# Late gates and their slot table moved ahead of the next unit's x on VectorE

## The chip, the cores and the metric

The kernel runs on one core of one Trainium2 chip. The metric is device time in microseconds of one execution, given as the median of several runs; lower is better. The kernel before takes 718.80 us (three runs: 718.79, 718.80 and 719.53).

## The reference

Three layers follow each other. Banded attention (4 batches, 8 heads, 576 positions, 64 channels; half of the heads see the last 32 positions, the others every fourth of the last 128) gives `x`, 2304 tokens by 512. A dense layer maps `x` through 2048 hidden units with a squared ReLU. A mixture of 8 experts then takes every token to the one expert with the largest logit and scales its output by a gate:

```python
logits = xn @ en.T / tau
expert_idx = np.argmax(logits, axis=1)
probs = np.exp(logits - logits.max(-1, keepdims=True))
probs /= probs.sum(-1, keepdims=True) + 1e-09
gate_w = probs[np.arange(N), expert_idx]
for e in range(E):
    mask = expert_idx == e
    h = np.maximum(x[mask] @ w1[e], 0.0)
    out[mask] = gate_w[mask, None] * (h @ w2[e])
```

(`xn` and `en` are the tokens and expert vectors divided by their norms; 512 inputs, 1024 hidden units for each expert.)

## The kernel before, in words

Attention and the dense layer take the first part of the span; tokens are worked on in five groups, and the last group (`g = 4`, four tiles of 128 tokens) is ready last. The routing decides which expert each token belongs to and sorts tokens into slots of 128 places. Slots are worked on in *units*: a pair of slots with one expert's weights, or a single slot. Unit 0 (slots 0 to 3, two passes) is formed early from the first four groups; all later units need the whole routing, which `slot_table` writes out as tables: which token is gathered into which place (`gidx`), where its output row goes (`sidx`), and its gate.

For one unit, `xt` transposes the gathered tokens on TensorE into a bank `px` (`x_turn`, L1123) and splits them into a high and a low half (`x_out`: ScalarE writes `xh`, L1135, VectorE `xl`, L1136). `g1_pair` multiplies them with the first weights into `ph` in four parts of 24 matmuls; ScalarE and VectorE make `hh` and `hl` of each part (L1159, L1160). `g2` multiplies those with the second weights into `po`, scales by the gate (L1205) and scatters the rows (L1206). Each matrix product is three matmuls of split operands (`mm3`, L468 to 470). The weights come as eight tiles `raw[k]` by DMA from the SyncE queue (L1084 for k under 4, L1086 for the others), and `split` turns each into `wh` (ScalarE, L1101) and `wl` (VectorE, L1102). A `raw[k]` is loaded again, for the next unit, when its `wl` is done.

The gates of the last group are made late, by `gates_late`: an inverse norm (L713 to 730), a product (L847), an Exp on ScalarE (L849), a sum (L850, L851), a reciprocal (L853) and the split of the gate into three bf16 numbers in `g3` (L854 to 857). Three products of the slot marks `eq` with the three rows of `g3` give `gb` (L919, 18 tiles by 25 places). 18 small matmuls on TensorE (`finish`, L925) sum `gb` into `pgate`, and a reduction (L928) gives the gate of each slot place. `finish` stands in TensorE's program between the last `g2` of unit 0 (slot 3) and the `g1` of unit 1 (slots 4 and 5).

TensorE runs its instructions in the order in which the code issues them. On VectorE and ScalarE a scheduler sets the order in this part of the program (after L1364 of the kernel before, in the loop over units, it is the code's order); `tc.issue_after(ins)` keeps what is issued under it behind `ins` on its engine. Each engine works its queue in order.

Of the kernel before, what the change touches and what calls it, by code (L numbers as in the profile page):

```python
# [11 lines left out]
AF = mybir.ActivationFunctionType  # L12
# [99 lines left out]
class Kern:  # L112
# [729 lines left out]
    def gates(self, g, ssq):  # L842
        nc, lp, n = self.nc, self.lpool, GT[g]
        sl = slice(T0[g], T0[g] + n)
        L = self.rel[:, sl, :]
        rn = self.inv_norm(lp, ssq[:, :n], n, f"yn{g}")
        nc.vector.tensor_mul(L, L, rn.unsqueeze(2).to_broadcast([P, n, NE]))  # L847
        z = lp.tile([P, 4], F32, tag="lz", name=f"lz{g}", bufs=2)[:, :n]
        nc.scalar.activation(L, L, AF.Exp)  # L849
        nc.vector.tensor_reduce(out=z, in_=L, axis=AX.X, op=ALU.add)  # L850
        nc.vector.tensor_scalar_add(z, z, 1e-9)  # L851
        gt = lp.tile([P, 4], F32, tag="lgt", name=f"lgt{g}", bufs=2)[:, :n]
        nc.vector.reciprocal(gt, z)  # L853
        nc.vector.tensor_copy(self.g3[:, 0, sl], gt)  # L854
        nc.vector.tensor_sub(z, gt, self.g3[:, 0, sl])
        nc.vector.tensor_copy(self.g3[:, 1, sl], z)
        nc.vector.tensor_sub(self.g3[:, 2, sl], z, self.g3[:, 1, sl])
# [6 lines left out]
    def bc(self, x, w):  # L864
        return x.unsqueeze(2).to_broadcast([P, x.shape[1], w])
# [17 lines left out]
    def slot_table(self, pos, nt, ns, nm):  # L883
        nc, pool, bc = self.nc, self.rpool, self.bc
        pi = pool.tile([P, 3, NTT], I32, tag="pi", name=f"pi{nm}")[:, :, :nt]
        pf = pool.tile([P, 2, NTT], F32, tag="pf", name=f"pf{nm}")[:, :, :nt]
        nc.vector.tensor_copy(pi[:, 0], pos)
        nc.vector.tensor_scalar(out=pi[:, 1], in0=pi[:, 0], scalar1=7, scalar2=None, op0=ALU.arith_shift_right)
        nc.vector.tensor_scalar(out=pi[:, 2], in0=pi[:, 0], scalar1=127, scalar2=None, op0=ALU.bitwise_and)
        nc.vector.tensor_copy(pf, pi[:, 1:3])  # L890
        eq = pool.tile([P, NTT * NPOS], F32, tag="eq", name=f"eq{nm}")[:, :nt * ns].rearrange("p (t j) -> p t j", t=nt)
        bt = pool.tile([P, NTT * 3 * NPOS], BF16, tag="bt", name=f"bt{nm}")[:, :nt * 2 * ns].rearrange(
            "p (t a j) -> p t a j", t=nt, a=2)
        nc.vector.tensor_tensor(out=eq, in0=bc(pf[:, 0], ns), in1=self.iota_j[:, :ns].unsqueeze(1).to_broadcast([P, nt, ns]),
                                op=ALU.is_equal)
        for i in range(2):
            nc.vector.tensor_mul(bt[:, :, i], eq, bc(self.dig[:, i, :nt], ns))
        pt = self.bank(f"ptab{nm}")
        at = pool.tile([P, NTT, P], BF16, tag="at", name=f"at{nm}")
        for t in range(nt):  # L900
            nc.vector.tensor_scalar(out=at[:, t], in0=self.iota_r, scalar1=pf[:, 1, t:t + 1], scalar2=None, op0=ALU.is_equal)
            nc.tensor.matmul(pt[:, 0:2 * ns], lhsT=at[:, t], rhs=bt[:, t].rearrange("p a b -> p (a b)"),
                             start=(t == 0), stop=(t == nt - 1))
        tb = pool.tile([P, 2, NPOS], F32, tag="tb", name=f"tb{nm}")[:, :, :ns]
        nc.vector.tensor_copy(tb, pt[:, 0:2 * ns].rearrange("p (a b) -> p a b", a=2))
        tk = pool.tile([P, NPOS], F32, tag="tk", name=f"tk{nm}")[:, :ns]
        nc.vector.scalar_tensor_tensor(out=tk, in0=tb[:, 0], scalar=64.0, in1=tb[:, 1], op0=ALU.mult, op1=ALU.add)
        gidx = pool.tile([P, ns], U32, name=f"gidx{nm}")
        self.last_gidx = nc.vector.tensor_scalar(out=gidx, in0=tk, scalar1=-1.0, scalar2=0.0, op0=ALU.add, op1=ALU.max)

        def rest():
            em = pool.tile([P, NPOS], F32, tag="em", name=f"em{nm}")[:, :ns]
            nc.vector.tensor_scalar(out=em, in0=tk, scalar1=0.0, scalar2=8192.0, op0=ALU.is_equal, op1=ALU.mult)
            sidx = pool.tile([P, ns], U32, name=f"sidx{nm}")
            nc.vector.scalar_tensor_tensor(out=sidx, in0=tk, scalar=-1.0, in1=em, op0=ALU.add, op1=ALU.add)
            gb = pool.tile([P, NTT * 3 * NPOS], BF16, tag="bt", name=f"gb{nm}")[:, :nt * 3 * ns].rearrange(
                "p (t a j) -> p t a j", t=nt, a=3)
            for i in range(3):
                nc.vector.tensor_mul(gb[:, :, i], eq, bc(self.g3[:, i, :nt], ns))  # L919
            return lambda: finish(sidx, gb)  # L920

        def finish(sidx, gb):
            pg = self.bank(f"pgate{nm}")
            for t in range(nt):
                nc.tensor.matmul(pg[:, 0:3 * ns], lhsT=at[:, t], rhs=gb[:, t].rearrange("p a b -> p (a b)"),  # L925
                                 start=(t == 0), stop=(t == nt - 1))
            gate = pool.tile([P, ns], F32, name=f"gate{nm}")
            nc.vector.tensor_reduce(out=gate, in_=pg[:, 0:3 * ns].rearrange("p (a b) -> p b a", a=3), axis=AX.X, op=ALU.add)  # L928
            return sidx, gate
        return gidx, rest  # L930
# [353 lines left out]
    def experts(self):  # L1284
        nc, tc = self.nc, self.tc
        w, xs, xts = self.w, self.xs, {}
# [6 lines left out]
        runs, place, n = [[]], {}, NEARLY  # L1293
# [39 lines left out]
        def gather(r):  # L1333
            for j in runs[r]:
                xs[j] = self.gather(j)

        def xt(r):
            xts[r] = self.xt(runs[r], [xs.pop(j) for j in runs[r]])
# [4 lines left out]
        gi, rest = tables()  # L1343
# [6 lines left out]
        part(3)  # L1350
        with tc.issue_after(self.last_gidx.ins):
            self.gates_late()
        self.g2(2, 0, *hts, w[0])
        xt(1)
        behind.append((self.last_xl,))
        for a in range(2):
            with ExitStack() as st:
# [3 lines left out]
                    self.split(1, k, w[1])  # L1361
        load_for(2)
        gather(2)
        rest = rest()  # L1364
        self.g2(3, 1, *hts, w[0])
        si, ga = rest()
        for j, p in place.items():
# [14 lines left out]
        with tc.manual_schedule(engines={mybir.EngineType.Activation, mybir.EngineType.DVE}):  # L1382
            raws, u = [self.raw, []], 1
            while u < nstat:
# [5 lines left out]
                ahead = None  # L1390
                for i in range(4):
                    if i == (u == 1):
                        if more:
                            ahead = self.x_turn(runs[u + 1], [xs.pop(j) for j in runs[u + 1]], True)
# [103 lines left out]
```

## Time and profile before

| | |
|---|---|
| time, median of 3 runs | 718.80 us |
| the profiled execution's own time | 719.62 us |
| its span, first to last instruction | 717.9 us |
| around the span | 1.7 us |
| TensorE busy in the span | 701.7 us, 98% |
| VectorE / ScalarE busy | 71% / 52% |
| mean granted TensorE clock | 0.994 of full |

Times in the profile are microseconds from the span's start. A busy share is an average; what a change in one stage is worth is read from that stage's rows. PE is TensorE's matmul, DVE is VectorE, ACT ScalarE, POOL GpSimd and SPq SyncE's queue of DMA issues. The idle time in square brackets is what an engine waited just before a group, with what ended it; a group with `x3` is three instructions in a row, with the time from the first one's start to the last one's end. TensorE's clock has two levels, 2.4 GHz (shown as 1.00) and 1.2 GHz (0.50).

### The profile page before, as it was taken

To read this page: it belongs to the slowest core of one execution; us is meant where nothing else is said; L and a number is where in the kernel's file an instruction comes from. 1 tells how busy PE (TensorE), PEld (TensorE's weight loads), DVE (VectorE), ACT (ScalarE), POOL (GpSimd) and SP (SyncE) were. 2 spreads that over 40 slices of the span, in tenths; PEclk is the share of its full clock that TensorE was granted. 3 is DMA by queue.
4 is the path that set the end of the run, shared out by engine and by line. 5 is a ranking of instruction groups with operands and counts; after the bars stand their busy time and mean duration, and the time that the engine had idled before them with its cause. 6 is when DMAs were issued, how large, how long until landed. Compare 5 with 4: busy or idle time off the path is not lost. (4 is left out here: it accounts for less than half of the span.)

```text
span 717.9 us, 13286 instructions
## 1 busy us (share of the span) xinstructions
PE 701.7 (98%) x4843; PEld 590.4 (82%) x4843; DVE 508.9 (71%) x1219; ACT 370.2 (52%) x828; POOL 59.6 (8%) x92
## 2 busy tenths in 40 slices
PE   9999999999999999999999999999979999999996
PEld 6677898787888888888888888888878989898884
DVE  6999998776776655887754879649846868686711
ACT  6899876764644433543434224451525656564510
POOL 5000000000000000000000000201510303031001
PEclk9999999999999999999999999999989999999999
DMA  9666754322211100212001004312640979796760
GB/s 277 212 197 197 218 172 155 122 79 77 96 54 59 55 23 8 89 54 60 23 1 58 1 1 172 122 60 89 225 158 16 315 234 331 232 325 223 244 254 32
DMA packets 37177, 95.50 MB, mean 133 GB/s; under 512 B 4454, under 2 KB 4454, under 8 KB 36976
## 3 DMA queue, kind: packets, MB, share of 16 engines
q1 hardware_dynamic: 33936, 84.61, 35.7%
q0 software_dynamic: 3168, 9.96, 3.9%
q8 instruction: 40, 0.66, 0.4%
q14 instruction: 33, 0.27, 0.1%
HBM read 92.46 MB, written 9.83 MB: 142 GB/s over the span
## 5 line engine op out<-in xcount | busy, mean ns | idle before, releaser
L468 PE MATMUL ph<-xhi,wih 128*128 128x512 f32 (+1 forms) x320 | 118.9, 372 | 0.0
L470 PE MATMUL ph<-xhi,wil 128*128 128x512 f32 (+1 forms) x320 | 117.8, 368 | 0.4 <-DVE wil L109 0.4
L469 PE MATMUL ph<-xlo,wih 128*128 128x512 f32 (+1 forms) x320 | 117.7, 368 | 0.2 <-DVE xlo L307 0.2
L468 PE MATMUL py<-woh,gh 128*128 128x512 f32 x288 | 115.3, 401 | 0.0
L470 PE MATMUL py<-woh,gl 128*128 128x512 f32 x288 | 112.5, 391 | 0.5 <-DVE gl L505 0.5
L469 PE MATMUL py<-wol,gh 128*128 128x512 f32 x288 | 112.6, 391 | 0.3 <-DVE wol L109 0.3
L1102 DVE TENSOR_TENSOR wl<-raw,wh 128x1024 fp32r<-128x1024 f32 x80 | 95.0, 1222 | 19.0 <-ACT wh L1101 19.0
L486 ACT ACTIVATE r<-ph 128x512 f32<-128x512 f32 (+1 forms) x80 | 44.1, 552 | 96.6 <-PE ph L470 96.2
L1101 ACT CAST wh<-raw 128x1024 fp32r<-128x1024 f32 x80 | 80.4, 1055 | 9.2 <-DMA raw<-in_moe_w 9.1
L769 DVE CUSTOM_DVE_ANT_0 junk<-ysb,enb 128x512 bf16<-128x512 f32 x112 | 77.0, 688 | 1.3
L507 DVE SCALAR_TENSOR_TENSOR gl<-r,sb,gh 128x512 fp32r<-128x512 f32 (+1 forms) x56 | 39.9, 713 | 53.5 <-ACT gh L496 53.5
L468 PE MATMUL ph<-xh,wh 128*128 128x256 f32 x256 | 73.7, 288 | 0.0
L496 ACT ACTIVATE gh<-r,sb 128x512 fp32r<-128x512 f32 (+1 forms) x56 | 38.7, 692 | 65.8 <-PE py L469 58.7
L469 PE MATMUL ph<-xl,wh 128*128 128x256 f32 x256 | 72.4, 283 | 0.0
L470 PE MATMUL ph<-xh,wl 128*128 128x256 f32 x256 | 72.3, 282 | 0.0
L468 PEld LDWEIGHTS ph<-xhi,wih 128*128 128x128 f32 x320 | 60.1, 188 | 11.3 <-ACT ysb L525 0.4
L470 PEld LDWEIGHTS ph<-xhi,wil 128*128 128x128 f32 x320 | 60.1, 188 | 11.0 <-DVE wil L109 1.0
L469 PEld LDWEIGHTS ph<-xlo,wih 128*128 128x128 f32 x320 | 60.1, 188 | 10.8 <-DVE xlo L307 0.6
L470 PEld LDWEIGHTS py<-woh,gl 128*128 128x128 f32 x288 | 54.1, 188 | 12.7 <-DVE gl L505 0.9
L468 PEld LDWEIGHTS py<-woh,gh 128*128 128x128 f32 x288 | 54.1, 188 | 11.5
L469 PEld LDWEIGHTS py<-wol,gh 128*128 128x128 f32 x288 | 54.1, 188 | 10.5 <-DVE wol L109 0.6
L468 PE MATMUL po<-wh,hh 128*128 128x512 f32 x152 | 59.8, 394 | 0.0
(334 smaller groups left out, 1241.8 us busy)
## 6 DMA issues: line engine op xcount, KB each, us to landing
raw<-in_moe_w SPq DMA_DIRECT2D x88, 512.0 KB
raw<-in_moe_w_in SPq DMA_DIRECT2D x16, 512.0 KB
raw<-in_moe_w_out SPq DMA_DIRECT2D x16, 512.0 KB
v<-in_vw SPq DMA_DIRECT2D x32, 192.0 KB
qk<-in_qkd SPq DMA_DIRECT2D x18, 320.0 KB
ydram<-ysb SPq DMA_DIRECT2D x18, 256.0 KB
raw_q<-in_moe_w SPq DMA_DIRECT2D x8, 512.0 KB
qk<-in_qkp SPq DMA_DIRECT2D x15, 272.0 KB
```

Source lines behind the costliest of these rows:

```text
L468: nc.tensor.matmul(out, lhsT=ah, rhs=bh, start=first, stop=False)
L469: nc.tensor.matmul(out, lhsT=ah, rhs=bl, start=False, stop=False)
L470: nc.tensor.matmul(out, lhsT=al, rhs=bh, start=False, stop=last)
L486: nc.scalar.activation(r, ph, AF.Relu)
L496: nc.scalar.activation(gh, r, AF.Identity, bias=self.sb[:, 1:2])
L507: nc.vector.scalar_tensor_tensor(out=gl, in0=r, scalar=self.sb[:, 1:2], in1=gh.bitcast(F32), op0=ALU.add, op1=ALU.subtract)
L769: ins = nc.vector.tensor_tensor_reduce(out=self.junk, in0=y, in1=self.enb[:, e], scale=1.0, scalar=0.0, op0=ALU.mult, op1=ALU.add, accum_o ...
L1101: nc.scalar.copy(h, r)
L1102: nc.vector.tensor_sub(l, r, h.bitcast(F32))
```

## The change

`rest()`, which issues `em`, `sidx` and the three products `gb`, is called right behind `gates_late()` and, as that, only kept behind the last `gidx`. The transposes of unit 1's x stay where they are. Their evacuation `x_out` (`xh`, `xl`) is kept behind the last `gb` and behind the Exp. The conversions `split` of `raw[4]` to `raw[7]` were kept behind the last `xl` and still are.

```diff
@@ gates
-        nc.scalar.activation(L, L, AF.Exp)
+        self.last_exp = nc.scalar.activation(L, L, AF.Exp)
@@ slot_table, rest
             for i in range(3):
-                nc.vector.tensor_mul(gb[:, :, i], eq, bc(self.g3[:, i, :nt], ns))
+                self.last_gb = nc.vector.tensor_mul(gb[:, :, i], eq, bc(self.g3[:, i, :nt], ns))
@@ experts
         with tc.issue_after(self.last_gidx.ins):
             self.gates_late()
+            rest = rest()
         self.g2(2, 0, *hts, w[0])
-        xt(1)
+        ahead = self.x_turn(runs[1], [xs.pop(j) for j in runs[1]])
+        with tc.issue_after(self.last_gb.ins), tc.issue_after(self.last_exp.ins):
+            xts[1] = self.x_out(runs[1], ahead)
         behind.append((self.last_xl,))
...
         load_for(2)
         gather(2)
-        rest = rest()
         self.g2(3, 1, *hts, w[0])
         si, ga = rest()
```

VectorE before, from the product of the last group's logits with the inverse norm on (`rel` holds the logits, `lz` their sums, `lgt` the gates, `wl_1` unit 1's low weights, `xl` its low x, `o` the output of unit 0's slot 3):

```order
L847 TENSOR_TENSOR rel<-rel,yn_r 128x32
L1136 TENSOR_TENSOR xl_5880<-px_5869,xh_5879 128x4x128
L1136 TENSOR_TENSOR xl_5880<-px_5874,xh_5879 128x4x128
L1102 TENSOR_TENSOR wl_1_5902<-raw_4937,wh_1_5901 128x1024
L850 TENSOR_REDUCE lz_5829<-rel 128x4
L1102 TENSOR_TENSOR wl_1_5906<-raw_4938,wh_1_5905 128x1024
L1102 TENSOR_TENSOR wl_1_5910<-raw_4939,wh_1_5909 128x1024
L1102 TENSOR_TENSOR wl_1_5914<-raw_4940,wh_1_5913 128x1024
L851 TENSOR_SCALAR lz_5829<-lz_5829 128x4
L1205 TENSOR_SCALAR o_5963<-po_5938,gatee 128x512
L853 RECIPROCAL lgt_5833<-lz_5829 128x4
```

VectorE after the change, from the end of the gates on; `L850`, `L851`, `L853` and `L854` now follow `L847` without anything between them, and these rows come next:

```order
L855 TENSOR_TENSOR lz_5829<-lgt_5833,g_1802 128x4
L919 TENSOR_TENSOR gbr<-eqr,g_1802 128x18x25
L856 CAST g_1802<-lz_5829 128x4
L857 TENSOR_TENSOR g_1802<-lz_5829,g_1802 128x4
L919 TENSOR_TENSOR gbr<-eqr,g_1802 128x18x25 x2
L1136 TENSOR_TENSOR xl_5888<-px_5877,xh_5887 128x4x128
L1136 TENSOR_TENSOR xl_5888<-px_5882,xh_5887 128x4x128
L1102 TENSOR_TENSOR wl_1_5910<-raw_4937,wh_1_5909 128x1024
L1102 TENSOR_TENSOR wl_1_5914<-raw_4938,wh_1_5913 128x1024
L1102 TENSOR_TENSOR wl_1_5918<-raw_4939,wh_1_5917 128x1024
L1102 TENSOR_TENSOR wl_1_5922<-raw_4940,wh_1_5921 128x1024
L1205 TENSOR_SCALAR o_5963<-po_5938,gatee 128x512
```

Two `xl`, four `wl` and the `o` that stood ahead of the gates' end and of `gb` now stand behind them.

ScalarE at the same place, before (`xh` is the high half of unit 1's x, `hh` the first hidden part of unit 1):

```order
L1101 CAST wh_1_5913<-raw_4940 128x1024
L1135 CAST xh_5879<-px_5869 128x4x128
L1135 CAST xh_5879<-px_5874 128x4x128
L849 ACTIVATE rel<-rel 128x32
L1159 ACTIVATE hh_5991<-ph_0_5993 128x512
```

and after the change:

```order
L1101 CAST wh_1_5921<-raw_4940 128x1024
L849 ACTIVATE rel<-rel 128x32
L1135 CAST xh_5887<-px_5877 128x4x128
L1135 CAST xh_5887<-px_5882 128x4x128
L1159 ACTIVATE hh_5991<-ph_0_5993 128x512
```

The Exp went ahead of the two `xh`; nothing else on ScalarE moved here.

GpSimd's queue of indirect DMAs at the same place (`x` are gathers for later units, `out` the scatters of unit 0's last two slots and unit 1's first), the difference with - before and + after:

```order
 L1206 DMA out<-o_5872,sidxe 2304x512
 L1108 DMA x_6387<-ydram,gidxr 128x512
+L1108 DMA x_6389<-ydram,gidxr 128x512
 L1206 DMA out<-o_5963,sidxe 2304x512
-L1108 DMA x_6389<-ydram,gidxr 128x512
 L1206 DMA out<-o_6172,sidxr 2304x512
```

One gather went ahead of the scatter of slot 3. TensorE's and SyncE's rows stand in the same order as before.

## Rows read from the trace of the kernel before

**Rows 1.** The page: busy time, share, instructions; granted clock in 40 slices

```profile
PE 701.7 (98%) x4843; PEld 590.4 (82%) x4843; DVE 508.9 (71%) x1219; ACT 370.2 (52%) x828; POOL 59.6 (8%) x92
...
PEclk9999999999999999999999999999989999999999
```

**Rows 2.** Waits of TensorE from 450 us on: total, times, longest

```profile
PE pgater L925 <- DVE gbr L919: 3.9, 1, 3.9
```

**Rows 3.** TensorE in stretches of 1 us: length, busy (count), granted clock, DMA share, GB/s

```profile
522.00:523.00 1.00, 0.00 (x0) 1.00 1.05 389
...
524.00:525.00 1.00, 0.00 (x0) 0.83 1.07 365
...
528.00:529.00 1.00, 1.00 (x7) 0.50 0.02 8
...
532.00:533.00 1.00, 1.00 (x12) 1.00 0.00 0
```

**Rows 4.** Timeline of TensorE around the wait: start, duration, line, operation, idle before

```profile
521.11 0.39 PE L470 MATMUL po<-wh,hl 128*128 128x512 f32 x1
525.35 1.30 PE L925 MATMUL pgater<-gbr,atr 128*128 128x75 bf16 x18 [3.85 <-DVE gbr L919]
526.45 0.56 PE L468 MATMUL ph<-xh,wh 128*128 128x256 f32 x1
...
531.62 0.60 PE L1123 MATMUL px<-ident,x 128*128 128x128 f32 x4
531.98 0.37 PE L468 MATMUL ph<-xh,wh 128*128 128x256 f32 x1
...
534.79 0.28 PE L468 MATMUL ph<-xh,wh 128*128 128x256 f32 x1
```

**Rows 5.** Timeline of TensorE at the slot table's own 18 small matmuls

```profile
503.52 0.63 PE L902 MATMUL ptabr<-btr,atr 128*128 128x50 bf16 x18
503.99 0.36 PE L468 MATMUL ph<-xh,wh 128*128 128x256 f32 x1
```

**Rows 6.** Timeline of VectorE, 516 to 526 us

```profile
516.08 0.19 DVE L847 TENSOR_TENSOR rel<-rel,yn_r 128x32 f32<-128x32 f32 x1
516.26 1.29 DVE L1136 TENSOR_TENSOR xl<-px,xh 128x512 fp32r<-128x512 f32 x2
517.47 1.22 DVE L1102 TENSOR_TENSOR wl<-raw,wh 128x1024 fp32r<-128x1024 f32 x1
...
518.69 3.49 DVE L1102 TENSOR_TENSOR wl<-raw,wh 128x1024 fp32r<-128x1024 f32 x3
...
522.17 0.75 DVE L1205 TENSOR_SCALAR o<-po,gatee 128x512 f32<-128x512 f32 x1
522.83 0.17 DVE L853 RECIPROCAL lgt<-lz 128x4 f32<-128x4 f32 x1
...
524.13 1.16 DVE L919 TENSOR_TENSOR gbr<-eqr,g 128x450 bf16<-128x450 f32 x2
```

**Rows 7.** Timeline of ScalarE, 515 to 549 us

```profile
515.64 1.07 ACT L1135 CAST xh<-px 128x512 fp32r<-128x512 f32 x2 [3.42 <-PE px L1123]
516.60 0.24 ACT L849 ACTIVATE rel<-rel 128x32 f32<-128x32 f32 x1
...
542.34 2.01 ACT L1101 CAST wh<-raw 128x1024 fp32r<-128x1024 f32 x2
548.61 0.60 ACT L1174 ACTIVATE h<-ph 128x512 f32<-128x512 f32 x1 [4.26 <-PE ph L470]
```

**Rows 8.** SyncE's DMA issues of unit 2's raw[4] to raw[7]

```profile
518.81 3.87 SPq L1086 DMA_DIRECT2D raw<-in_moe_w  x4
```

**Rows 9.** Timeline of GpSimd, 517 to 533 us

```profile
517.12 1.02 POOL L1206 DMA_INDIRECT out<-o,sidxe  x1 [0.30 <-DVE xl L1136]
518.45 1.09 POOL L1108 DMA_INDIRECT x<-ydram,gidxr  x1 [0.31 <-issue]
...
532.49 0.97 POOL L1108 DMA_INDIRECT x<-ydram,gidxr  x1 [7.66 <-PE px L1123]
```

## The prediction

> **What bounds the kernel now.** I read the page's busy shares first: TensorE is busy 98% of the span, every other engine far less [rows 1]. So a microsecond counts where TensorE stands still or runs slowly, and almost nowhere else. The second view is the list of TensorE's waits, cut to the expert part: from 450 us on it has a single entry, the small gate matmuls waiting 3.9 us for VectorE's `gb` [rows 2]. After it TensorE waits for nobody until its work ends. The third view is the granted clock. The page's line shows one dip in the expert part [rows 1], and stretches of 1 us place it: TensorE stands at full clock while idle in 522 to 523, falls in 524 to 525, is at 0.50 (1.2 GHz) in 528 to 529 although it is busy again, and is back at 1.00 in 532 to 533 [rows 3]. The wait therefore has two prices, the idle time and the half-speed matmuls behind it.
>
> The timeline of VectorE says why `gb` is late. The last product is ready at 524.13 + 1.16 = 525.29, and the gate matmuls start at 525.35 [rows 4, 6]. VectorE is not short of work before that: between L847 (ending 516.27) and the reciprocal L853 (522.83) it does two `xl`, four `wl` and the `o` of slot 3 [rows 6]. The `o` even waits for the matmul just ahead of the gate matmuls in TensorE's queue (521.11 [rows 4]), so before the change `gb` could not have been in time.
>
> **The change part by part.** It adds no instruction and removes none; it reorders VectorE and ScalarE.
>
> *When `gb` is ready now.* L847 still ends at 516.27: all ahead of it is unchanged but for `em` and `sidx`, which moved a few places while TensorE had work. Exp follows on ScalarE, 0.24 us [rows 7]; ScalarE loses nothing by letting it go first but the start of `xh`, which slips from 515.64 to about 516.6. A hand-over between engines took 0.06 us above (525.29 to 525.35). So the logits are back at about 516.6. L850 and L851 are as small as L853 (0.17 us); at 0.2 us a step that is 517.0. From L853 to the last product took 525.29 − 522.83 = 2.46 us with nothing foreign between [rows 6]. `gb` is ready at about 519.5, and if every hand-over cost 0.3 us, at 520.0. TensorE's last matmul of slot 3 ends at 521.11 + 0.39 = 521.50 [rows 4]. Spare: 1.5 to 2 us. The wait is gone.
>
> *What is late next.* `xl` was done at 517.55 and now comes behind `gb`: 519.5 + 1.29 = 520.8 [rows 6]. TensorE wants it behind the gate matmuls, at about 522.05 (below), 1.2 us later. `xh` is done by 516.6 + 1.07 = 517.7 [rows 7]. Both hidden. The four `wl` take 1.22 + 3.49 = 4.7 us [rows 6] and end at 525.5 where they ended at 522.18; they serve unit 1's second product, which stands behind four parts of 24 matmuls (2.81 us each, below), not before 533. The `o` of slot 3 and the gate's reduction slip to about 526.5. The first `hl` of unit 1 can then be 0.7 us late, but TensorE has three `ph` banks and comes back to this one three parts later.
>
> *Loads behind it.* A `raw[k]` is loaded again when its `wl` is done, so these four issues move from 518.81 (the last about 522.7 [rows 8]) to 522.1 and 526. The old set had landed by 528, where the DMA share falls to 0.02 [rows 3]: 5.3 us behind its last issue. The new one lands by 531.3. ScalarE's first cast of it stands at 542.34 before [rows 7] and about 535.5 after the gain. Spare 4 us.
>
> *GpSimd's queue.* The scatter of slot 3 now stands behind the gather `x_6389`, which waits for unit 2's first transposes (531.62 [rows 4], its issue at 532.49 [rows 9]; both some 7 us earlier after the change). The scatter slips about 3 us, to 526.7. No engine reads what it writes, and its tile is written again only by the second output of unit 1.
>
> *The sum.* Idle time: 3.85 us [rows 4]; it is 4.0 if the gate matmuls may start, as others do, while the one before drains. The gate matmuls took 526.45 − 525.35 = 1.10 us at half clock. No row shows them at full clock; the nearest is the slot table's 18 matmuls with 50 columns for 75, 503.99 − 503.52 = 0.47 us [rows 5], and half of 1.10 is 0.55. I take 0.55, a saving of 0.55 (bounds 0 with no change and 0.63). The first part of unit 1, 24 matmuls, ran from 526.45 to 531.62, 5.17 us, nearly all at half clock; the next 24 ran from 531.98 to 534.79, 2.81 us, at full clock [rows 4]. Saving 2.36. Together 3.85 + 0.55 + 2.36 = **6.8 us**, bounds 6.2 and 7.0.
>
> *Is it given back later?* Behind 532 TensorE waits for nothing [rows 2], and weights, hidden parts and gathers there follow TensorE's own progress, so they move along. The profiled execution took 719.62 and would take 712.8. The runs' median is 718.80, 0.8 lower with the same program; 718.8 − 6.8 = **712.0 us**.
>
> *A rule weighed.* While `gb` is made now, GpSimd issues a scatter at 517.12 (1.02 us) and a gather at 518.45 (1.09 us) [rows 9]. In the trace the gather lies beside three `wl`, which also read two operands, and these took 3.49 / 3 = 1.16 us each, no more than the single one's 1.22 [rows 6]: no hold is seen. The Trainium skill, "SBUF — State Buffer", section "Who interferes with whom", says that a VectorE instruction with two SBUF inputs contends with a GpSimd instruction that reads SBUF and that one then blocks for the other's whole length. By the trace the sum stays; by the rule it is the first rival.
>
> **The rivals.**
> 1. *VectorE is held by GpSimd's descriptor work.* If the products stood still for both, 1.02 + 1.09 = 2.1 us, `gb` is ready at 521.6 and `xl` at 522.9, 0.8 us after TensorE wants it. For: the overlap in time is new for `gb`. Against: the unstretched `wl`. Time 712.8.
> 2. *The clock falls although the idle time is gone*, for a cause other than the wait. Then only the 3.85 us are gained: 715.0. For: the fall lies where the DMAs are at their busiest (1.07 [rows 3]). Against: it comes only after TensorE has stood idle, and it ends once TensorE has been busy again.
> 3. *Slower: the reloads of raw[4] to raw[7] come too late.* They start 3.3 us later and are wanted 6.8 us earlier. If the first landed after 535.5, ScalarE's queue would stand, and behind the casts stands the ReLU of the next `g1`, for which ScalarE has 4.26 us of idle time ahead [rows 7]. So TensorE stalls from a landing at 539.8 on, and once the stall is as long as today's, 3.85 us, the clock loss of 2.9 us returns as well. Slower than before is a landing past 543.7, some 21.5 us behind its issue; at 25 us (547.1) the stall is 7.3 us and the time 712.0 + 7.3 + 2.9 = 722.2. Against: the whole old set was in 9.2 us behind its first issue [rows 3, 8].
> 4. *It does not do what it says*: another entry holds the gate matmuls at the same place, and the time stays at 718.8. Against: the order rows show all inputs of `gb` ahead of the old obstacles, and the other operand of the gate matmuls, `at`, is the one that the slot table's matmuls used already at 503.52 [rows 5].
>
> **How the numbers follow.** Forecast 82 in 100, 712.0, own range 711.4 to 713.0 (the bounds of the sum and 0.4 us for the spread of runs). Rival 1: 6; rival 2: 6; rival 3: 3; rival 4: 3. The range that should hold the time 8 times in 10 takes the forecast and rival 1, and 0.8 us beyond these for a small wait that I have not seen: 711.0 to 713.8. A measurement of this kernel can tell about 0.2%, 1.4 us, from no change; the forecast and rivals 1 and 2 are faster by more: 0.94; rival 4 gives 0.03 for no change, rival 3 gives 0.03 for slower.
>
> **What would show it.** Right: the gate matmuls start within 0.3 us of the last matmul of slot 3, near 521.5, and take about 0.55; the entry in TensorE's waits is gone; the granted clock stays at 1.00 from 520 to 535; the first 24 matmuls of unit 1 take about 2.8 us; `gb` ends near 519.5 and `xl` near 520.8; the four issues stand near 522 to 526; TensorE ends its work near 703.5. Wrong: a wait of the first `ph` for `xl` (rival 1), a clock of 0.50 behind a gate matmul that did not wait (rival 2), or a wait of ScalarE for `raw` near 536 (rival 3).

## The result and the profile after

The changed kernel takes **713.18 us** (median of 6 runs, 712.69 to 713.47) where the kernel before takes 718.84 (6 runs on the same chip, 718.51 to 719.64): ratio 0.9918, 95% interval 0.9905 to 0.9931 (the pairs of figures behind the ratios below are such intervals), a gain of 5.7 us. The profiled execution took 713.13 us with a span of 711.3; the one of before took 719.62 and 717.9, 6.5 us more.

TensorE's list of waits from 450 us on is empty now; the entry of [rows 2] is gone. The page of the changed kernel, busy time and granted clock in 40 slices:

```profile
PE 698.4 (98%) x4843; PEld 587.2 (83%) x4843; DVE 508.3 (71%) x1219; ACT 370.2 (52%) x828; POOL 58.8 (8%) x92
...
PEclk9999999999999999999999999999999999999998
```

The dip of the clock in the expert part [rows 1] is gone too; the 8 at the end is the idle tail. The timeline of TensorE in the changed kernel:

```profile
521.08 0.39 PE L470 MATMUL po<-wh,hl 128*128 128x512 f32 x1
521.31 0.83 PE L925 MATMUL pgater<-gbr,atr 128*128 128x75 bf16 x18
521.97 0.36 PE L468 MATMUL ph<-xh,wh 128*128 128x256 f32 x1
...
524.80 0.60 PE L1123 MATMUL px<-ident,x 128*128 128x128 f32 x4
525.16 0.37 PE L468 MATMUL ph<-xh,wh 128*128 128x256 f32 x1
```

Set beside [rows 4]: the gate matmuls start 0.23 us behind the start of slot 3's last matmul, the spacing of a queue that runs; they take 0.66 us to the next start where they took 1.10, and the first part of unit 1 takes 2.83 us where it took 5.17. Unit 2's transposes stand at 524.80, not at 531.62: 6.8 us earlier. VectorE:

```profile
516.04 0.19 DVE L847 TENSOR_TENSOR rel<-rel,yn_r 128x32 f32<-128x32 f32 x1
516.53 0.19 DVE L850 TENSOR_REDUCE lz<-rel 128x4 f32<-128x32 f32 x1 [0.29 <-ACT rel L849]
...
518.27 1.16 DVE L919 TENSOR_TENSOR gbr<-eqr,g 128x450 bf16<-128x450 f32 x2
519.34 1.28 DVE L1136 TENSOR_TENSOR xl<-px,xh 128x512 fp32r<-128x512 f32 x2
520.54 4.62 DVE L1102 TENSOR_TENSOR wl<-raw,wh 128x1024 fp32r<-128x1024 f32 x4
525.08 0.74 DVE L1205 TENSOR_SCALAR o<-po,gatee 128x512 f32<-128x512 f32 x1
525.74 0.22 DVE L928 TENSOR_REDUCE gater<-pgater 128x25 f32<-128x75 f32 x1
525.88 0.68 DVE L1160 SCALAR_TENSOR_TENSOR hl<-ph,hh 128x512 fp32r<-128x512 f32 x1
```

`gb` is ready at 519.43, `xl` at 520.62, both ahead of TensorE's need. The first `hl` starts 0.2 us after its `hh` (525.06 + 0.60 below), which nothing waits for. ScalarE's timeline in the changed kernel:

```profile
516.27 0.23 ACT L849 ACTIVATE rel<-rel 128x32 f32<-128x32 f32 x1 [4.08 <-DVE yn_r L730]
516.40 1.06 ACT L1135 CAST xh<-px 128x512 fp32r<-128x512 f32 x2
525.06 0.60 ACT L1159 ACTIVATE hh<-ph 128x512 fp32r<-128x512 f32 x1 [7.60 <-PE ph L470]
...
535.52 2.01 ACT L1101 CAST wh<-raw 128x1024 fp32r<-128x1024 f32 x2
```

SyncE's reloads of raw[4] to raw[7] in the changed kernel:

```profile
521.88 3.77 SPq L1086 DMA_DIRECT2D raw<-in_moe_w  x4
```

GpSimd's timeline in the changed kernel, with the gather beside `gb` and the two that changed places:

```profile
518.42 1.32 POOL L1108 DMA_INDIRECT x<-ydram,gidxr  x1 [0.30 <-issue]
525.99 0.95 POOL L1108 DMA_INDIRECT x<-ydram,gidxr  x1 [6.26 <-PE px L1123]
527.25 1.50 POOL L1206 DMA_INDIRECT out<-o,sidxe  x1 [0.30 <-issue]
```

The reloads start 3.1 us later than in [rows 8], and the casts that read them start 6.8 us earlier than in [rows 7], without a wait for a DMA. The scatter of slot 3 (527.25) slipped behind the gather, and nothing waits for it. Stretches of TensorE (length, busy and count, granted clock, DMA share, GB/s) show why, and that the clock stays up:

```profile
524.00:525.00 1.00, 1.00 (x11) 1.00 1.01 389
...
530.00:531.00 1.00, 1.00 (x11) 1.00 0.49 188
531.00:532.00 1.00, 1.00 (x11) 1.00 0.02 8
```

The DMAs of these loads are done by 531, over 4 us ahead of the first cast (535.52). The DMA share at 524 (1.01) is near the 1.07 at which the clock fell before [rows 3]; the clock is 1.00.

### The profile page after: what moved, and what is told of

It is laid out like the page before. It is cut to its first block, busy times and chain, and to the rows that moved or that the text cites. A ratio compares the mean times of both kernels' runs of the same rounds, so it can differ in the third digit from the quotient of the medians.

```text
span 711.3 us, 13285 instructions
## 1 busy us (share of the span) xinstructions
PE 698.4 (98%) x4843; PEld 587.2 (83%) x4843; DVE 508.3 (71%) x1219; ACT 370.2 (52%) x828; POOL 58.8 (8%) x92
```

## The experiments

Theory: the gain is TensorE's wait, in two terms, the idle time and the half-speed matmuls behind it. Open after the result: why the medians moved 1.1 us less than the rows of the first profile said (6.8).

**The kernel before and the changed kernel, unchanged.** No edit.

> The kernel before once more, unchanged, with the span and granted clock of each of its runs and a second profile. The change gained 5.7 us by the medians but 6.5 between the two profiled executions. Theory (the loss in the wait differs from execution to execution, since the return of the clock does): the runs spread over about 1 us, the slower ones at the lower mean clock; two profiles show the idle time at 3.8 to 4.0 us in both, and the half-clock stretch behind it at different lengths, worth 2.1 to 3 us. Rival (the spread has nothing to do with the wait): clock the same in all runs to 0.0005, and the half-clock stretch as long as in the first profile, 2.9 us lost, with the difference elsewhere.

> The changed kernel once more, unchanged. Theory: 712.7 to 713.5 us, 0.7 to 0.8% under the kernel before on the same chip, no wait of TensorE at the gate matmuls, clock 1.00 from 520 to 535. In the first profile the last small matmuls of the quarters (raw_q) took 2.3 us where those of before took 1.9; if that is a spread of executions, this profile or the other one shows the other value; if the change does it, 2.3 again here and 1.9 in every kernel with the old order.

Measured: before again 718.98 us (11 runs, ratio to the same kernel 1.0002, 0.9993 to 1.0011; the 18 runs beside it have a median of 718.39); after again 712.80 (5 runs, 712.37 to 713.40), ratio 0.992, 0.9907 to 0.9934, and in its profile TensorE's list of waits from 450 us on is empty again and the granted clock is 1.00 from 520 to 535. The 29 runs of the kernel before on this chip fall into two groups by their granted clock:

| mean granted clock of the run | runs | median us |
|---|---|---|
| 0.993, 0.994 | 14 | 719.15 |
| 0.995, 0.996 | 15 | 718.25 |

The second profile of before is from the second group (718.19 us, clock 0.995), the first one (719.62, 0.994) from the first. TensorE's timeline in the second profile of before:

```profile
525.22 1.18 PE L925 MATMUL pgater<-gbr,atr 128*128 128x75 bf16 x18 [3.84 <-DVE gbr L919]
...
530.30 0.60 PE L1123 MATMUL px<-ident,x 128*128 128x128 f32 x4
```

and its stretches of 1 us:

```profile
525.00:526.00 1.00, 0.78 (x15) 0.71 1.07 383
526.00:527.00 1.00, 1.00 (x11) 0.50 1.00 391
...
529.00:530.00 1.00, 1.00 (x11) 1.00 0.00 0
```

The wait is the same, 3.84 us. From the gate matmuls to the transposes it takes 5.08 us where the first profile had 6.27 [rows 4] and the changed kernel has 3.49. So the clock term is 1.6 us here and 2.8 there, with the same program and the same idle time. The theory holds, though 1.6 lies below the 2.1 to 3 us that were expected; the rival, equal clock terms, falls. The two profiled executions are 1.4 us apart (719.62 and 718.19), and 1.2 of it lies behind the wait. The mean granted clock is taken over the whole span, so in the table it is a sign of that stretch and not a measure of it. The medians of the two samples of before, 718.39 and 718.98, differ by 0.6 us with the same kernel on the same chip: 8 of the 11 runs of the one are from the slower group, but 6 of the 18 of the other.

The other question is the last small matmuls of the quarters. TensorE's timeline in the first profile of the changed kernel:

```profile
696.45 2.38 PE L1247 MATMUL po<-raw_q,quarters 128*32 128x128 f32 x64
```

and in its second one:

```profile
696.64 1.93 PE L1247 MATMUL po<-raw_q,quarters 128*32 128x128 f32 x64
```

1.93 us is also what both profiles of before have. The longer time is not the change's doing: a kernel with the old order of VectorE has it too, the one of the last experiment below:

```profile
703.25 2.37 PE L1247 MATMUL po<-raw_q,quarters 128*32 128x128 f32 x64
```

The profiles of the longer and the shorter wait have 2.38 and 2.39 us as well, those of the run that keeps TensorE busy and of the moved gate matmuls 1.93. The last three experiments ran on another chip than the four ahead of them; whether that is the cause stays open.

**TensorE kept busy while it waits.**

```diff
             pg = self.bank(f"pgate{nm}")
+            if nm == "r":
+                self.busy(pg, 18, self.ones)
```

> The kernel before with the old order of VectorE, and 18 dummy matmuls (128x512 bf16, into the bank that the gate matmuls then overwrite) ahead of the gate matmuls, some 3.9 us at full clock, so that TensorE stays busy while it waits for gb. Theory (the clock falls because TensorE stands idle): gb as late as before, gate matmuls at about 525.4, but the clock stays at 1.00; the gate matmuls take about 0.6 us and the first part of unit 1 2.8 us, and the time falls by the clock term alone, 2.1 to 2.9 us: 716.0 to 716.7. Rival (the clock falls for the DMA burst of those microseconds): clock 0.50 behind it all the same, time 718.8, not under 718.4.

Measured: 716.68 us (8 runs), before on the same chip 718.39; ratio 0.9975, 0.9964 to 0.9985. VectorE's last two products `gb`, and TensorE's timeline (lines from L925 on stand two lower than before):

```profile
524.41 1.16 DVE L919 TENSOR_TENSOR gbr<-eqr,g 128x450 bf16<-128x450 f32 x2
```


```profile
521.62 4.06 PE L312 MATMUL pgater<-ones 128*128 128x512 bf16 x18
525.62 0.82 PE L927 MATMUL pgater<-gbr,atr 128*128 128x75 bf16 x18
...
529.09 0.60 PE L1125 MATMUL px<-ident,x 128*128 128x128 f32 x4
```

and a stretch of TensorE:

```profile
526.00:527.00 1.00, 1.00 (x19) 1.00 1.08 420
```

`gb` is as late as before (525.57; 525.29 before) and the DMAs as busy (1.08), but the clock stays at 1.00 and the gate matmuls and the first part take 3.47 us. So it was TensorE's idling that brought the clock down here, and not the DMAs. The time is in the expected range, but before stood at 718.39 on this chip, so the gain is 1.7 us (1.9 by means), 0.4 under the lower end that was expected; the changed kernel gains another 3.9 us on the same chip (716.68 − 712.80), which is the idle time.

**The gate matmuls moved in TensorE's queue, VectorE's order as before.**

```diff
-        si, ga = rest()
-        for j, p in place.items():
-            self.sidx[j], self.gate[j] = si[:, p:p + 1], ga[:, p:p + 1]
...
                     part(i, h)
+                    if u == 1 and i == 1:
+                        si, ga = rest()
+                        for j, p in place.items():
+                            self.sidx[j], self.gate[j] = si[:, p:p + 1], ga[:, p:p + 1]
```

> The kernel before with the old order of VectorE and ScalarE, and the gate matmuls moved in TensorE's own queue behind the second part of unit 1, with the gate's reduction behind them. Theory (the loss is TensorE's queue standing at the gate matmuls, whoever is late): the first part of unit 1 starts at about 521.4, gb is ready at 525.3 and wanted at 527.5, no wait, clock 1.00, time as the changed kernel's within 0.3 us: 712.8 to 713.5. Rival (the new order of VectorE gains by itself, by xl, wl or the loads): at most half of the gain, 716 or more.

Measured: 712.73 us (5 runs, 712.42 to 713.04), ratio 0.9917, 0.9904 to 0.9931; the changed kernel took 712.80 beside it. VectorE has its last two products `gb` where they were in the kernel before, ready at 525.14:

```profile
523.98 1.16 DVE L919 TENSOR_TENSOR gbr<-eqr,g 128x450 bf16<-128x450 f32 x2
```

TensorE's timeline has the gate matmuls at full speed and without a wait:

```profile
524.00 0.60 PE L1123 MATMUL px<-ident,x 128*128 128x128 f32 x4
...
527.18 0.83 PE L925 MATMUL pgater<-gbr,atr 128*128 128x75 bf16 x18
```

The whole gain comes with VectorE's order as before, but for the gate's reduction, which moved along with the gate matmuls. What counts here is that nothing in TensorE's queue stands ahead of ready work and waits; the rival, a gain by `xl`, `wl` or the loads, falls.

**A longer wait.**

```diff
-            for i in range(3):
+            for i in ([0] * 7 if nm == "r" else []) + [0, 1, 2]:
                 nc.vector.tensor_mul(gb[:, :, i], eq, bc(self.g3[:, i, :nt], ns))
```

> The kernel before with the first of the three products gb made seven times more, with the same result (0.55 us each on VectorE), so that gb comes some 3.85 us later and TensorE waits some 7.7 us. It tells the two prices of the wait apart by doubling one. Theory (idle time counts one for one, the clock is lost once): the time rises by the added idle time alone, to 722.2 us (721.9 to 722.6), with a half-clock stretch behind the wait that costs 1.5 to 2.9 us as before. Rival (the clock term grows with the wait): the time rises by 5.5 us or more, to over 723.5.

Measured: 723.59 us (6 runs, 722.32 to 723.88) against 719.05; ratio 1.0054, 1.0042 to 1.0066. TensorE's timeline:

```profile
529.50 1.30 PE L925 MATMUL pgater<-gbr,atr 128*128 128x75 bf16 x18 [8.03 <-DVE gbr L919]
...
535.21 0.60 PE L1123 MATMUL px<-ident,x 128*128 128x128 f32 x4
```

The wait grew by 4.2 us (8.03 against 3.85), 0.3 more than meant, and the time by 4.5 by the medians and 4.1 by the means, with an interval of 3.0 to 4.7. The median lies above the rival's 723.5, but that number goes by a kernel before at some 718 us; on this chip it is at 719.05, so the expected 722.2 becomes 722.9 and the rival's 5.5 us would be 724.5. What decides is the profile: the stretch behind the wait takes 5.71 us, a clock term of 2.2, within the 1.6 to 2.8 of the two profiles of before, though the wait is twice as long. Within this spread the idle time counts one for one and the clock is lost once.

**A shorter wait.** In the changed kernel, `xl` and three `wl` go back ahead of `gb`:

```diff
-        nc.vector.tensor_sub(l, r, h.bitcast(F32))
+        self.last_wl = nc.vector.tensor_sub(l, r, h.bitcast(F32))
...
-            rest = rest()
...
-        with tc.issue_after(self.last_gb.ins), tc.issue_after(self.last_exp.ins):
+        with tc.issue_after(self.last_exp.ins):
             xts[1] = self.x_out(runs[1], ahead)
...
                 for k in range(4 * a, 4 * a + 4):
+                    if k == 7:
+                        with tc.issue_after(self.last_wl.ins):
+                            rest = rest()
+                        st.enter_context(tc.issue_after(self.last_gb.ins))
                     self.split(1, k, w[1])
...
-        self.g2(3, 1, *hts, w[0])
+        with tc.issue_after(self.last_gb.ins):
+            self.g2(3, 1, *hts, w[0])
```

> The changed kernel with the two xl and three of the four conversions wl put back ahead of gb; the o of slot 3 and the last wl stay behind it. gb should be ready at about 524 and TensorE idle 2.4 to 2.8 us. If the wait is priced one for one and the clock does not fall: 712.8 + 2.6 = 715.4 us. If the clock falls here too: about 717.1 us. Rival (what the change gains is gained by xl and the conversions being out of the way and not by the wait): no relation to the idle time; 712.8 or 718.4.

Measured: 716.60 us (6 runs) against 719.05, ratio 0.9961, 0.9948 to 0.9975; but the median hides two groups: 715.65, 715.81 and 715.96 us at a mean clock of 0.997 to 0.998, and 717.25, 717.46 and 717.57 at 0.995 to 0.996. The profile is from the second group; TensorE's timeline:

```profile
523.96 0.95 PE L925 MATMUL pgater<-gbr,atr 128*128 128x75 bf16 x18 [2.46 <-DVE gbr L919]
...
529.02 0.60 PE L1123 MATMUL px<-ident,x 128*128 128x128 f32 x4
```

and a stretch of TensorE:

```profile
525.00:526.00 1.00, 1.00 (x6) 0.50 1.04 397
```

Both expected cases came about, each in three runs, 1.6 us apart and each some 0.4 us above its expected time, on a chip where the kernel before is 0.7 us above its time on the other one. The rival, no relation to the idle time, falls. Behind the wait it took 5.06 us, a clock term of 1.6. The gate matmuls start at 523.96, and the clock falls only in the stretch behind that (0.74 from 524 to 525): the price can begin after the wait has ended. That the first group kept its clock is read from the runs' mean clock alone, and no profile shows it.

**The early call alone.**

```diff
         with tc.issue_after(self.last_gidx.ins):
             self.gates_late()
+            rest = rest()
...
-        rest = rest()
```

> One part of the change alone: the slot table's second half is called early, right behind the gates, but x_out is not kept behind gb and the Exp. The scheduler then gives VectorE and ScalarE the order of the kernel before. Theory (the gain is the order that the two fences set): wait of 3.8 to 4.0 us, time 718.0 to 719.6, as before. Rival (calling it early is enough): 713.

Measured: 719.06 us (10 runs), ratio 1.000, 0.9991 to 1.0009. The wait is where it was:

```profile
525.33 1.30 PE L925 MATMUL pgater<-gbr,atr 128*128 128x75 bf16 x18 [3.85 <-DVE gbr L919]
```

The call's place in the code does nothing by itself; it takes the two fences, which keep `x_out` behind `gb` and the Exp, to make the order. Which of the two is needed is not shown: neither was tried alone.

## Why the prediction was right, and where it was off

- *What bounds, and the wait that goes.* Right: the only wait of TensorE in the expert part, gone in the result, and worth the gain by itself, since moving the gate matmuls gives the same.
- *When `gb` is ready* (519.5): 519.43. *What is late next* (`xl` at 520.8, `wl` at 525.5): 520.62 and 525.16. The gate's reduction ended at 525.96, predicted 526.5.
- *Loads and GpSimd's queue.* Issues at 521.88 to 525.65, landed by 531, no wait of ScalarE; the scatter stands at 527.25, predicted 526.7, and nobody waited.
- *The sum in the rows.* Idle time 4.04 us (gate matmuls at 521.31, before at 525.35; predicted 3.85, upper bound 4.0), gate matmuls 0.44 (predicted 0.55), first part 2.34 (predicted 2.36): 6.8 us, as predicted. The profiled executions differ by 6.5; the 0.45 us that the small matmuls of the quarters took longer in the profile of the changed kernel account for the difference and a little more. TensorE's last matmul ended at 704.12 + 0.39 = 704.51; the 703.5 of the prediction was a slip, since by the sum its work ends at 710.41 + 0.39 − 6.8 = 704.0, and the 0.45 us make the rest.
- *The step that was off* is the last of the sum: "718.8 − 6.8 = 712.0". The 6.8 contain a clock term of 2.8 us that belongs to the profiled execution; the same program loses 1.6 in the other profile, and its runs lie in two groups 0.9 us apart. The profiled execution was 0.8 above the median, and the other profile puts most of such a difference (1.2 of 1.4 us) behind the wait: I took the full term off a median that contains less of it. Taken off its own execution, 719.62 − 6.8 = 712.8, the sum is 0.3 from the 713.13 of the changed kernel's profile. A clock term of about 1.7 us, as the run that kept TensorE busy (1.7) and the two groups of the shorter wait (1.6) measure it, and 3.9 to 4.0 of idle time make the 5.6 to 5.7 of the medians. So the time, 713.18, lies outside the forecast's own range (711.4 to 713.0) and inside the wide one (711.0 to 713.8) by the room left for rival 1 and for a small wait, neither of which came about; that part was luck. It is also nearer to rival 1's 712.8 than to 712.0, and the rows, not the time, tell the two apart.
- *Rival 1* (VectorE held by GpSimd) fell, and its argument that the overlap is new for `gb` was wrong. In the kernel before GpSimd issues the scatter of slot 3 beside the products `gb`, so the 2.46 us of the prediction had such an issue in them:

```profile
523.51 1.32 POOL L1206 DMA_INDIRECT out<-o,sidxe  x1 [3.98 <-DVE lz L855]
```

The last two products took 1.16 us there [rows 6], 1.16 us in the changed kernel with the gather beside them, and 1.16 us in the run with the shorter wait, where no issue of GpSimd lies beside them (from 520.3 to 526.3). The Trainium skill, "SBUF — State Buffer", section "Who interferes with whom", says that a VectorE instruction with two SBUF inputs contends with a GpSimd instruction that reads SBUF. VectorE's times show nothing of it here. GpSimd's issues took 1.32 us beside `gb` and 0.97 to 1.09 in [rows 9], but one of 1.50 (527.25 in the changed kernel) lies beside a `wl`, so the longer time is not shown to come from `gb`.

- *Rival 2* (the clock falls anyway) fell with the run that kept TensorE busy. *Rivals 3 and 4* did not come about.

## What to carry to other kernels

A small product that waits in an in-order TensorE queue costs its wait and, when the clock falls, the half speed behind it, so read both: the idle time, and the matmuls behind it at half speed. The cure may stand in either queue: the producer's order or the consumer's place gave the same time here (712.80 and 712.73 us). And the term that comes from the clock varied from execution to execution here (1.6 to 2.8 us): subtract it from the execution it was read in, and look at the runs' clocks before you carry it to a median.

## What the runs showed of the hardware

- The same idle time of 3.84 and 3.85 us cost 1.6 us of half speed in one execution and 2.8 in another, and an idle time of 2.46 us lowered the clock in at least one of six executions, by the mean clock in three. The Trainium skill, "TensorE: Matmul & The Clock Gate", section "What's actually happening", says that the moment at which the clock rises varies from run to run; the two profiles of before agree, with the clock back at 1.00 in the stretch from 532 [rows 3] in one and from 529 in the other. The fall varies in them too: it lies in the stretch from 524 (0.83 [rows 3]) in one and from 525 (0.71) in the other.
- The products `gb` took 1.16 us for two with an issue of GpSimd beside them and without one. GpSimd's own issues of an indirect DMA took 0.94 to 1.50 us between 515 and 530 us of the span in the two kernels; what sets this stays open.
